# Agent attention and a routed MoE in one kernel: leftover rows read in place, row copies due later, queries and keys at other steps

## The chip, the cores and the metric

The kernel runs on one core of one Trainium2 chip, in one launch. The metric is the device time of the execution in microseconds (us). Three runs of the kernel before took 1318.40, 1320.83 and 1327.73 us; the median is 1320.83 us. The execution that was profiled took 1319.42 us, and its span from the first to the last instruction was 1317.7 us.

TensorE (PE) multiplies matrices, VectorE (DVE), ScalarE (ACT) and GpSimd (POOL) work on elements, and SyncE (SP) issues nearly all transfers of this kernel, one after the other in its program order. PEld is the load of a weight into PE, and it overlaps PE.

## The reference

There are 4 batches of 11456 tokens with 128 features, 49 agents for each batch, and 8 experts with 1024 hidden units.

```
scale = 1/sqrt(128)
def sm(a, b):                      # softmax over the last axis
    s = scale * (a @ b.T);  s = s - s.max(-1);  e = exp(s)
    return e / (e.sum(-1) + 1e-9)

agent_v = sm(agents, k) @ v        # 49 x 128 for a batch
x       = sm(q, agents) @ agent_v  # 11456 x 128 for a batch

logits = x @ w_gate                # all 45824 tokens
e      = argmax(logits);  g = softmax(logits)[e]
out    = g * (relu(x @ w1[e]) @ w2[e])
```

All inputs and the output are float32.

## The kernel before, in words

**Chunks, groups and steps.** A batch has 12 chunks: 11 of 1024 tokens (8 tiles of 128), and one of 192 tokens (2 tiles of 96). A chunk has up to two groups of 512 tokens, 23 groups in a batch. A group is worked off in 8 steps, one for each 128 hidden units, so that a batch takes 184 steps and a full chunk 16. The step is the unit of the kernel's own timetable.

**What a step does.** Most tokens of a batch are routed to one expert; its first weight is folded with `agent_v`, so that the first layer is a product of the exponentials of the query scores with a matrix `W` of 128 rows. The exponentials of the 49 agents are kept as float16 pairs, a high and a low part. The 128 rows that PE contracts at once (a tile `M`) hold 49 + 49 rows of the pair, and in the 30 left the high parts again, for the low part of the weight. The other 19 agents' high parts do not fit. For them there is a second, small product with 19 rows (`Wq`), in four groups of rows that start at rows 0, 32, 64 and 96: function `rests`, L1190, one group for each of four hidden tiles. Its input `Q` was four copies of 19 rows of `M` (L602). Then L1198 adds the product with 128 rows, ACT (L1203) and DVE (L1204) write the hidden units as a pair `hh`, and 5 steps later 12 matmuls (L1217) add them to the output `py`. After 8 steps DVE scales the group (`yo`, L1230) and SP stores it (issued by a helper's line, L1293).

**From queries to `M`.** A chunk of queries is loaded (L277), split into float16 pairs by ACT (L337) and DVE (L339), turned over by a transposing transfer `hT<-hl` on SP (L361), and multiplied with the agents on PE (L388 to L390). `qscores` and `qexp` (DVE L573, ACT L578) make the exponentials `E`, which SP also stores (`exps<-E`, L1293). `esplit` writes the pair into one of two buffers `mm` (DVE L584, ACT L585, DVE or POOL L587), `eturn` turns it over with another transposing transfer `M<-mm` (L593), `rest` issues the four copies `Q<-M`, and `logits` multiplies `M` with the gate's weights on PE (L610), for the routing. Keys of the next batch take the same way up to their scores, and stand beside the queries of the batch at hand.

**What sets the order.** The program is written out by a table of events: `at(t, f)` puts a function at step t, `after(dt, f)` puts it dt steps later than now. Each engine then works in its program order. The constants are steps. Queries of chunk c start at QA + 8c (first three chunks) and then every 13 steps (10.5 in the last batch), relative to the batch's step 0. Their scores come 9 steps later (KL), `esplit` another 3, and `logits` LL = 9.5 steps after the scores (LLL = 11 in the last batch). `rest` follows `eturn` by DTQ = 3.5 steps. Stores of `E` and of `yo` come DEX = 2 and DST = 2 steps after they are written. Keys of a next batch start at step -208 + 10c relative to that batch, which is step -24 + 10c of the batch at hand. For the second batch the first three keys thus stood ahead of step 0 of the first.

PSUM has 8 banks; six are for scores, logits and the first layer (`ph`, `ps_small`), two for `py`. There are 6 buffers of `M`, 3 of `Q`, and 2 of `hT` for keys and for queries each.

## Time and profile before

| what | us |
|---|---|
| median of three runs | 1320.83 |
| the profiled execution | 1319.42 |
| its span | 1317.7 |
| up to the first step of the first batch | 111 |
| the 736 steps of four batches | 111 to 1258 |
| blocks of tokens routed elsewhere, after that | 1258 to 1318 |

Times in the rows are from the start of the span. Busy time of an engine is a union of its instructions; PE's is stretched where its granted clock is low. A wait is idle time of an engine before an instruction, put down to what ended it. All of SP's work is issuing, so its rows in the timeline show how long the queue was taken by each issue.

### The profile page before, as it was taken

The page shows a single profiled execution, that of the slowest core. Times are in us where ns is not written, and L with a number is a line of the kernel's source. Part 1 is how long each engine was busy: PE and PEld are TensorE (multiplying, and loading weights), DVE is VectorE, ACT ScalarE, POOL GpSimd, SP SyncE. Part 2 cuts the span into 40 slices and gives each one's busy share as a digit, 9 for nine tenths or more (in the row PEclk, how much of TensorE's full clock was granted, in tenths as well). Part 3 has the DMA queues.
Part 4 walks back from the last instruction along what each step waited for, and adds up shares of the span by engine and source line. Part 5 has one row for each costly group of instructions (what it writes and reads, how often), then busy time and mean ns, then how long its engine had stood idle before and what let it go on. Part 6 is the DMA issues. An engine that isn't in the chain of part 4 may idle for free.

```text
span 1317.7 us, 35023 instructions
## 1 busy us (share of the span) xinstructions
PE 1074.8 (82%) x14238; PEld 832.7 (63%) x14238; DVE 1000.1 (76%) x2454; ACT 773.1 (59%) x1393; POOL 138.8 (11%) x198
## 2 busy tenths in 40 slices
PE   8626778789986877888987776888998879989995
PEld 8514557667764755666765665666775656667795
DVE  3677767687796786687887785768797968979985
ACT  4457646465486574566476583556476545666682
POOL 0200000032000000021200000012200012210123
PEclk9767888889997797999997797878998979988998
DMA  8769998643298798844189999743156576443270
GB/s 323 212 165 198 230 175 172 102 134 81 88 245 164 143 217 157 186 124 113 39 259 159 174 192 192 163 118 90 36 188 120 95 129 148 82 140 121 70 252 15
DMA packets 269813, 197.94 MB, mean 150 GB/s; under 512 B 218313, under 2 KB 231106, under 8 KB 269648
## 3 DMA queue, kind: packets, MB, share of 16 engines
q1 hardware_dynamic: 267792, 192.36, 63.2%
q0 software_dynamic: 1568, 2.25, 1.0%
q8 instruction: 113, 1.85, 0.6%
q10 hardware_dynamic: 288, 1.05, 0.3%
q14 instruction: 52, 0.43, 0.1%
HBM read 99.75 MB, written 36.43 MB: 103 GB/s over the span
## 4 chain that ended last, share of the span: by engine, by line
PE 34%; DMA 22%; DVE 21%; ACT 10%; issue 8%; SPq 3%; POOL 2%; POOLq 0%; ACTq 0%; DVEq 0%
PE py L1217 16%; DVE hh L1204 8%; PE ph L1198 7%; DMA M<-mm 7%; DMA ld<-in_q_dram 4%; PE ph L1190 4%; ACT hh L1203 3%; DMA wn<-in_moe_w_dram 3%; DMA hT<-hl 3%; DVE hl L339 2%; PE ps_small L478 2%; ACT jk L321 2%; DVE S L450 2%; DMA ld<-in_k_dram 2%; ACT hl L337 2%
## 5 line engine op out<-in xcount | busy, mean ns | idle before, releaser
L1217 PEld LDWEIGHTS <-hh 128*128 128x128 f16 x8640 | 584.5, 104 | 115.3 <-issue 40.0
L1217 PE MATMUL py<-w2h,hh 128*128 128x128 f16 (+1 forms) x5760 | 649.9, 229 | 1.4 <-ACT hh L1203 1.0
L1203 ACT ACTIVATE hh<-ph 128x512 f16<-128x512 f32 (+1 forms) x728 | 415.2, 585 | 304.1 <-PE ph L1198 275.0
L1204 DVE SCALAR_TENSOR_TENSOR hh<-ph,hh 128x512 f16<-128x512 f32 (+1 forms) x736 | 482.2, 669 | 145.4 <-ACT hh L1203 141.2
L1217 PE MATMUL py<-w2l,hh 128*128 128x128 f16 (+1 forms) x2880 | 559.5, 228 | 0.0
L1198 PE MATMUL ph<-M,W 128*128 128x512 f16 (+1 forms) x736 | 298.3, 409 | 0.0
L1190 PE MATMUL ph<-Q,Wq 19*128 19x512 f16 (+1 forms) x736 | 128.4, 401 | 90.0 <-DVE hh L1204 64.2
L1198 PEld LDWEIGHTS <-W 128*128 128x128 f16 x736 | 74.2, 102 | 115.0 <-issue 114.0
L321 ACT ACTIVATE jk<-ld 128x1024 f16<-128x1024 f32 (+1 forms) x84 | 84.8, 1010 | 56.7 <-DMA ld<-in_q_dram 35.8
L339 DVE SCALAR_TENSOR_TENSOR hl<-ld,mul,hl 128x1024 f16<-128x1024 f32 (+1 forms) x84 | 101.3, 1211 | 3.8 <-ACT hl L337 3.7
L337 ACT ACTIVATE hl<-ld,mul 128x1024 f16<-128x1024 f32 (+1 forms) x84 | 91.1, 1095 | 19.1 <-DMA hT<-hl 12.9
L388 PE MATMUL ps_small<-agh,hT 128*128 128x49 f16 (+1 forms) x630 | 62.9, 191 | 24.4 <-DMA hT<-hl 24.4
L587 POOL TENSOR_TENSOR mm<-E,mm 128x392 f16<-128x392 f32 (+1 forms) x18 | 14.7, 817 | 618.6 <-DVE mm L584 390.5
L1190 PEld LDWEIGHTS <-Wq 19*128 19x128 f16 x736 | 27.9, 92 | 80.6 <-issue 41.7
L610 PE MATMUL ps_small<-Gs,M 128*128 128x18 f16 x360 | 17.0, 174 | 74.8 <-DMA M<-mm 74.0
L388 PEld LDWEIGHTS <-hT 128*128 128x128 f16 (+1 forms) x630 | 56.0, 102 | 28.0 <-DMA hT<-hl 25.6
L610 PEld LDWEIGHTS <-M 128*128 128x128 f16 x360 | 14.0, 101 | 79.0 <-DMA M<-mm 78.2
L1230 DVE TENSOR_TENSOR yo<-py,cs 128x512 f32<-128x512 f32 (+1 forms) x92 | 61.4, 667 | 1.8 <-PE py L1217 1.6
L389 PE MATMUL ps_small<-agl,hT 128*128 128x49 f16 (+1 forms) x630 | 62.2, 190 | 0.0
L390 PE MATMUL ps_small<-agh,hT 128*128 128x49 f16 (+1 forms) x630 | 62.0, 190 | 0.0
L389 PEld LDWEIGHTS <-hT 128*128 128x128 f16 (+1 forms) x630 | 55.0, 102 | 1.6 <-issue 1.5
L390 PEld LDWEIGHTS <-hT 128*128 128x128 f16 (+1 forms) x630 | 54.3, 101 | 0.0
(295 smaller groups left out, 1313.1 us busy)
## 6 DMA issues: line engine op xcount, KB each, us to landing
ld<-in_k_dram SPq DMA_DIRECT2D x44, 512.0 KB
ld<-in_v_dram SPq DMA_DIRECT2D x44, 512.0 KB
ld<-in_q_dram SPq DMA_DIRECT2D x44, 512.0 KB
out_dram<-yo SPq DMA_DIRECT2D x88, 256.0 KB
w1e<-in_moe_w_dram SPq DMA_DIRECT2D x17, 512.0 KB
w2e<-in_moe_w_dram SPq DMA_DIRECT2D x17, 512.0 KB
exps<-E SPq DMA_DIRECT2D x44, 196.0 KB
wn<-in_moe_w_dram SPq DMA_DIRECT2D x16, 512.0 KB
```

The costliest lines, as they stand in the source:

```text
L321: nc.scalar.activation(jk[:p, :t * D], x[:p, :t, :].rearrange("p t d -> p (t d)"), AF.Square, accum_out=ss[:p])
L337: nc.scalar.activation(hi[:p, :t, :], x[:p, :t, :], AF.Copy, scale=m)
L339: nc.vector.scalar_tensor_tensor(lo[:p, :t, :], x[:p, :t, :], m, hi[:p, :t, :], op0=ALU.mult, op1=ALU.subtract)
L388: nc.tensor.matmul(o, x[:, 0, i, :p], AG["h"], start=True, stop=False)
L389: nc.tensor.matmul(o, x[:, 0, i, :p], AG["l"], start=False, stop=False)
L390: nc.tensor.matmul(o, x[:, 1, i, :p], AG["h"], start=False, stop=True)
L1190: nc.tensor.matmul(ph[:, :nn], st['Wq'][k, f0 // 4, :], st['Q'][c][k, h:h + n, :chunks[c][1]], start=True, stop=False)
L1198: nc.tensor.matmul(ph[:, :nn], st['W'][:, f, :], st['M'][c][:, h:h + n, :chunks[c][1]], start=False, stop=True)
L1203: nc.scalar.activation(hh[:, 0, :nn], ph[:, :nn], AF.Relu)
L1204: nc.vector.scalar_tensor_tensor(hh[:, 1, :nn], ph[:, :nn], 0.0, hh[:, 0, :nn], op0=ALU.max, op1=ALU.subtract)
L1217: mm_ = lambda l, r, **k: nc.tensor.matmul(o, l, r, skip_group_check=True, **k)
L1230: nc.vector.tensor_tensor(yo[:p, :n, :], py[:p, :n * D].rearrange("p (i d) -> p i d", d=D), cs.unsqueeze(2).broadcast_to([p, n, D]), op=AL ...
```

## The change

The 128 rows of `mm` are laid out anew: low parts in columns 0 to 48, high parts in columns 66 to 114 (UP = 66), and the 30 repeated high parts in two pieces, columns 49 to 65 (agents 0 to 16) and 115 to 127 (agents 17 to 29). Agents 30 to 48 thus lie in rows 96 to 114 of `M`, where the fourth row group of the small product reads its input in place. `rest` issues three copies, from rows 96 to 114, and has its own event: 9 steps (QD) ahead of the chunk's first step, or later. ACT repeats the 30 columns in two casts; the folded matrix `av` and the masks of rows follow the new layout.

The timetable changes too: queries 6 steps sooner (QA -20 to -26); LL 9.5 to 14 and LLL 11 to 15; DEX 2 to 4 and DST 2 to 5; and the keys of the second batch at step 3 + 7.6c of the first (KS1).

```diff
--- before.py
+++ after.py
@@ -22,6 +22,8 @@
 P = 128
 A = 49
 KR = 128 - 2 * A
+UP = 96 - KR
+DUP = ((A, 0, UP - A), (UP + A, UP - A, KR))
 CH = 1024
 BIG = float(1 << 20)
 UNROLL = 4
@@ -47,13 +49,13 @@
 VE, T1, TF0, TF1, TL, TLM, Q0 = 12, 1.75, 3, 1.5, 18, 10, 2
 
 KS, KT, VT, VL, VL4, TW0, TW1, DW = -208, 10, 4, 4, 4, 8, 2.5, 1
-QA, QB, QC, QB3, KL, LL, RG, D1, DL = -20, 8, 13, 10.5, 9, 9.5, 0.7, 0.5, 0
-
-KS1 = []
-
-KLL, LLL = 11, 11
-
-DTR, DTE, DTQ, DEX, DST, DXS = 2, 0.5, 3.5, 2, 2, 0.5
+QA, QB, QC, QB3, KL, LL, RG, D1, DL = -26, 8, 13, 10.5, 9, 14, 0.7, 0.5, 0
+
+KS1 = [3 + 7.6 * c for c in range(12)]
+
+KLL, LLL = 11, 15
+
+DTR, DTE, QD, DEX, DST, DXS = 2, 0.5, 9, 4, 5, 0.5
 
 LAG = 5
 
@@ -123,10 +125,14 @@
     pidx = cpool.tile([P, 1], F32, name="pidx")
     nc.gpsimd.iota(itmp[:, 0:1], pattern=[[0, 1]], base=0, channel_multiplier=1)
     nc.vector.tensor_copy(pidx, itmp[:, 0:1])
+    restrow = cpool.tile([P, 1], F32, name="restrow")
+    for o, a0, a1 in DUP:
+        nc.vector.tensor_scalar(itmp[:, 1:2].bitcast(F32), pidx, float(o), None, op0=ALU.is_ge)
+        nc.vector.tensor_scalar(itmp[:, 2:3].bitcast(F32), pidx, float(o + a1 - a0), None, op0=ALU.is_ge)
+        nc.vector.tensor_tensor(itmp[:, 3 + (a0 > 0):4 + (a0 > 0)].bitcast(F32), itmp[:, 1:2].bitcast(F32), itmp[:, 2:3].bitcast(F32), op=ALU.subtract)
+    nc.vector.tensor_tensor(restrow, itmp[:, 3:4].bitcast(F32), itmp[:, 4:5].bitcast(F32), op=ALU.add)
     sumrow = cpool.tile([P, 1], F32, name="sumrow")
-    nc.vector.tensor_scalar(sumrow, pidx, float(2 * A), None, op0=ALU.is_lt)
-    restrow = cpool.tile([P, 1], F32, name="restrow")
-    nc.vector.tensor_scalar(restrow, pidx, float(2 * A), None, op0=ALU.is_ge)
+    nc.vector.tensor_scalar(sumrow, restrow, -1.0, 1.0, op0=ALU.mult, op1=ALU.add)
     eidx = cpool.tile([P, E], F32, name="eidx")
     itmp2 = cpool.tile([P, E], I32, name="itmp2")
     nc.gpsimd.iota(itmp2, pattern=[[1, E]], base=0, channel_multiplier=0)
@@ -502,9 +508,10 @@
                 av = wpool.tile([P, P], F32, tag="av", name="av")
                 pt = small_ps()
                 nc.tensor.matmul(pt[:, :A], AV["acc"][:64 + A], both[:64 + A], start=True, stop=True)
-                nc.vector.tensor_tensor(av[:, :2 * A].rearrange("p (j a) -> p j a", a=A), pt[:, :A].unsqueeze(1).broadcast_to([P, 2, A]),
-                                        rs.unsqueeze(1).broadcast_to([P, 2, A]), op=ALU.mult)
-                nc.vector.tensor_copy(av[:, 2 * A:], av[:, :KR])
+                nc.vector.tensor_tensor(av[:, :A], pt[:, :A], rs, op=ALU.mult)
+                nc.vector.tensor_copy(av[:, UP:UP + A], av[:, :A])
+                for o, a0, a1 in DUP:
+                    nc.vector.tensor_copy(av[:, o:o + a1 - a0], av[:, a0:a1])
                 avq = one.tile([P, 4, 32], F32, tag="avq", name="avq")
                 nc.gpsimd.memset(avq, 0.0)
                 nc.gpsimd.tensor_copy(avq[:, :, :A - KR], av[:, KR:A].unsqueeze(1).broadcast_to([P, 4, A - KR]))
@@ -581,10 +588,12 @@
         def esplit(c):
             _, p, t = chunks[c]
             e, m2 = Es[c], mm[c % len(mm)]
-            nc.vector.tensor_copy(m2[:p, :t, :A], e[:p, :t, :])
-            nc.scalar.copy(m2[:p, :t, 2 * A:], e[:p, :t, :KR])
+            up = m2[:p, :t, UP:UP + A]
+            nc.vector.tensor_copy(up, e[:p, :t, :])
+            for o, a0, a1 in DUP:
+                nc.scalar.copy(m2[:p, :t, o:o + a1 - a0], e[:p, :t, a0:a1])
             eng = nc.gpsimd if pick(M2L if last else M2E, c) == "P" else nc.vector
-            eng.tensor_tensor(m2[:p, :t, A:2 * A], e[:p, :t, :], m2[:p, :t, :A], op=ALU.subtract)
+            eng.tensor_tensor(m2[:p, :t, :A], e[:p, :t, :], up, op=ALU.subtract)
             after(0 if first and c == 0 else DTE, eturn, c, m2)
 
         def eturn(c, m2):
@@ -592,14 +601,13 @@
             m = mpool.tile([P, 8, P], F16, tag="M", name="M")
             nc.sync.dma_start_transpose(m[:, :t, :p], m2[:p, :t, :].rearrange("p t a -> p (t a)"))
             Ms[c] = m
-            after(0 if first and c == 0 else DTQ, rest, c)
 
         def rest(c):
 
             _, p, t = chunks[c]
             x = Qs[c] = mpool.tile([P, 8, P], F16, tag="Q", name="Q", bufs=MQ)
-            for r in range(4):
-                nc.sync.dma_start(x[32 * r:32 * r + A - KR, :t, :p], Ms[c][KR:A, :t, :p])
+            for r in range(3):
+                nc.sync.dma_start(x[32 * r:32 * r + A - KR, :t, :p], Ms[c][96:96 + A - KR, :t, :p])
 
         def logits(c):
             _, p, t = chunks[c]
@@ -806,6 +814,7 @@
             at(base + t + ql_ + 3, esplit, c)
             tl = max(t + ql_ + (TL if first and c < NQ else LLL if last and c > 2 else LL), ta + (TLM if first else 4) + c / 2)
             at(base + tl, logits, c)
+            at(base + max(c * 16 - QD, t + ql_ + 6.5), rest, c)
             if c + 1 in starts or c == NCK - 1:
                 turns(route(c), base + tl + 1, RG, 6)
                 tf = max(tl + 1 + 6 * RG, tw + 1)
@@ -1187,7 +1196,8 @@
             for r in range(4):
                 k = slice(32 * r, 32 * r + A - KR)
                 ph = phs[g, f0 + r] = psH.tile([P, 512], F32, tag="h", name="ph")
-                nc.tensor.matmul(ph[:, :nn], st['Wq'][k, f0 // 4, :], st['Q'][c][k, h:h + n, :chunks[c][1]], start=True, stop=False)
+                nc.tensor.matmul(ph[:, :nn], st['Wq'][k, f0 // 4, :], st['Q' if r < 3 else 'M'][c][k, h:h + n, :chunks[c][1]],
+                                 start=True, stop=False)
 
         def layer1(g, f):
             c, h, n = groups[g]
```

Lines behind the first piece of the diff move by 6 to 10: L361 becomes L367, L388 L394, L593 L602, L602 L610, L610 L618, L1190 L1199, L1198 L1208, L1293 L1303.

How the program's order moves shows at two places. The first is PE at the start, from the last logits of the first batch's first three chunks (`Gs,M`) to its first step (`Wq`, `W`). Before:

```order
L610 MATMUL ps_small<-Gs,M 128x18
L293 MATMUL ps_small<-sa,ones 128x1
L303 MATMUL ps_small<-ident,ag 128x49
L388 LDWEIGHTS hT
L388 MATMUL ps_small<-agh,hT 128x49
L389 LDWEIGHTS hT
L389 MATMUL ps_small<-agl,hT 128x49
L390 LDWEIGHTS hT
L390 MATMUL ps_small<-agh,hT 128x49
```

and so on through two chunks of keys (48 matmuls), and only then the first step. In the change:

```order
L618 MATMUL ps_small<-Gs,M 128x18
L1199 LDWEIGHTS Wq
L1199 MATMUL ph<-Q,Wq 128x512
L1199 LDWEIGHTS Wq
L1199 MATMUL ph<-Q,Wq 128x512
L1199 LDWEIGHTS Wq
L1199 MATMUL ph<-Q,Wq 128x512
L1199 LDWEIGHTS Wq
L1199 MATMUL ph<-M,Wq 128x512
L1208 LDWEIGHTS W
L1208 MATMUL ph<-M,W 128x512
```

The keys' scores have gone behind the first step, and the fourth small product reads `M`.

The second is SP in the second batch, about the sixth chunk of queries, from its `exps` to the next. Before:

```order
L1293 DMA exps<-E 128x392
L1293 DMA out_dram<-yo 128x512
L593 DMA_TRANSPOSE M<-mm_137 128x8x128
L361 DMA_TRANSPOSE hT<-hl 128x16x128
L602 DMA Q<-M 19x1024 x4
L277 DMA ld<-in_q_dram 96x256
L277 DMA ld<-in_v_dram 128x1024
L1293 DMA out_dram<-yo 128x512
```

In the change:

```order
L1303 DMA exps<-E 128x392
L602 DMA_TRANSPOSE M<-mm_143 128x8x128
L367 DMA_TRANSPOSE hT<-hl 128x16x128
L610 DMA Q<-M 19x1024
L367 DMA_TRANSPOSE hT<-hl 128x16x128
L610 DMA Q<-M 19x1024
L1303 DMA out_dram<-yo 128x512
L610 DMA Q<-M 19x1024
```

The store no longer stands between the exponentials and `M<-mm`, and the copies are three, apart from each other, with a transpose between them. Over the whole program, counted in these rows, 29 of the 77 transposes `hT<-hl` that stand for a whole chunk had copies `Q<-M` among the transfers since the transpose ahead of them; now 38 have.

## Rows read from the trace of the kernel before

**Rows 1.** The page's first part: busy time of three engines (share of the span) and their instructions.

```profile
PE 1074.8 (82%) x14238; PEld 832.7 (63%) x14238; DVE 1000.1 (76%) x2454; ACT 773.1 (59%) x1393; POOL 138.8 (11%) x198
```

**Rows 2.** Stretches of the span, by batch: length, busy us of PE, PEld, DVE, ACT and POOL with counts, granted clock (share of 2.4 GHz), DMA share, GB/s.

```profile
0.00:111.00 111.00, 59.44 (x630) 54.24 (x630) 63.84 (x211) 54.33 (x92) 10.17 (x24) 0.76 0.80 223
111.00:400.00 289.00, 243.25 (x3338) 186.24 (x3336) 219.84 (x501) 178.28 (x323) 27.26 (x45) 0.91 0.71 161
400.00:700.00 300.00, 248.54 (x3375) 189.70 (x3375) 230.75 (x545) 181.78 (x329) 26.08 (x44) 0.90 0.70 157
700.00:1000.00 300.00, 250.55 (x3326) 190.77 (x3326) 227.94 (x539) 178.58 (x320) 26.54 (x43) 0.87 0.65 143
1000.00:1258.00 258.00, 229.29 (x2858) 168.96 (x2858) 217.09 (x596) 148.32 (x281) 30.07 (x28) 0.91 0.51 110
```

**Rows 3.** What PE waited for over the whole span: us in total, times, longest us.

```profile
PE ps_small L610 <- DMA M<-mm: 74.0, 23, 7.3
PE ph L1190 <- DVE hh L1204: 64.2, 52, 7.1
...
PE ph L1190 <- DMA Q<-M: 14.5, 10, 5.0
```

**Rows 4.** The same view for the stretches 111 to 400, 400 to 700, 700 to 1000 and 1000 to 1258 us, in this order: PE's waits for `M` ahead of the logits.

```profile
PE ps_small L610 <- DMA M<-mm: 13.9, 5, 5.4
...
PE ps_small L610 <- DMA M<-mm: 21.8, 6, 5.6
...
PE ps_small L610 <- DMA M<-mm: 21.8, 5, 7.3
...
PE ps_small L610 <- DMA M<-mm: 8.4, 5, 3.3
```

**Rows 5.** Timeline of PE ahead of the first step: start us, us, what, and in brackets the idle time before it and what ended that.

```profile
91.92 0.34 PE L303 MATMUL ps_small<-ident,ag 49*128 49x49 f32 x1
107.21 0.22 PE L388 MATMUL ps_small<-agh,hT 128*128 128x49 f16 x1 [14.95 <-DMA hT<-hl]
...
109.94 0.22 PE L388 MATMUL ps_small<-agh,hT 128*128 128x49 f16 x1 [1.55 <-DMA hT<-hl]
...
111.06 0.61 PE L1190 MATMUL ph<-Q,Wq 19*128 19x512 f16 x4
```

**Rows 6.** Timeline of the same stretch on SP (two rows) and on DVE (one row, the last weight of the second layer).

```profile
78.94 3.03 SPq L602 DMA_DIRECT2D Q<-M  x4
...
95.50 11.80 SPq L361 DMA_TRANSPOSE hT<-hl  x2
```

```profile
86.64 1.28 DVE L743 SCALAR_TENSOR_TENSOR w2l<-w2e,pinv,w2h 128x1024 f16<-128x1024 f32 x1
```

**Rows 7.** Timeline of SP in the second batch, without a row left out: start us, us that the issue took, what.

```profile
478.07 0.41 SPq L1293 DMA_DIRECT2D out_dram<-yo  x1
478.52 6.37 SPq L361 DMA_TRANSPOSE hT<-hl  x1
484.94 1.52 SPq L277 DMA_DIRECT2D ld<-in_v_dram  x3
486.56 5.50 SPq L361 DMA_TRANSPOSE hT<-hl  x1
492.14 0.53 SPq L1293 DMA_DIRECT2D exps<-E  x1
492.76 0.38 SPq L1293 DMA_DIRECT2D out_dram<-yo  x1
493.25 1.29 SPq L593 DMA_TRANSPOSE M<-mm  x1
494.59 2.64 SPq L361 DMA_TRANSPOSE hT<-hl  x1
497.32 2.45 SPq L602 DMA_DIRECT2D Q<-M  x4
```

**Rows 8.** Timeline of the same chunk on the other engines: the last part of `esplit` (POOL), the logits (PE), and the group `yo` (DVE) whose store is the first of rows 7.

```profile
485.19 0.91 POOL L587 TENSOR_TENSOR mm<-E,mm 128x392 f16<-128x392 f32 x1 [43.39 <-DVE mm L584]
```

```profile
496.70 0.39 PE L610 MATMUL ps_small<-Gs,M 128*128 128x18 f16 x8 [5.59 <-DMA M<-mm]
```

```profile
465.48 0.68 DVE L1230 TENSOR_TENSOR yo<-py,cs 128x512 f32<-128x512 f32 x1
```

**Rows 9.** Instructions by line: count, shortest/median/longest ns, first and last start in us. The first row holds one matmul for each step.

```profile
L1198 PE MATMUL ph<-M,W x736: 242/379/634, 111.6 to 1257.9; 128*128 128x512 f16 x176, 128*128 128x192 f16 x8
```

```profile
L602 SPq DMA_DIRECT2D Q<-M x192: 561/562/1129, 78.9 to 1217.0; - x192
```

```profile
L585 ACT CAST mm<-E x48: 230/384/466, 74.4 to 1160.9; 128x240 f16<-128x240 f32 x44, 96x60 f16<-96x60 f32 x4
```

**Rows 10.** One copy of `av`'s columns on DVE (timeline), and a copy `Q<-M` on the chain of waits (start us, us to its landing).

```profile
58.39 0.17 DVE L507 COPY av<-av 128x30 f32<-128x30 f32 x1
```

```profile
399.84 6.02 DMA Q<-M
```

## The prediction

> **What bounds the kernel now.** I read the busy times first, then the stretches by batch, then PE's waits, and last SP's timeline where PE waits. No engine is full: PE is busy 82% of the span, DVE 76%, ACT 59% [rows 1]. In the second and third batch PE works 249 and 251 of 300 us, DVE 231 and 228 [rows 2], so each loses some 50 us in gaps. PE's list of waits names them: 74.0 us in 23 waits for `M` ahead of the logits, 64.2 us in 52 short waits for a `ph` bank that DVE's `hh` gives back, and 14.5 us for `Q` [rows 3]. The first of these lies, but for 8 us ahead of the first step, in the four batches: 13.9, 21.8, 21.8 and 8.4 us, together 65.9 us [rows 4].
>
> Why `M` is late is read off one chunk. `esplit` ends at 485.19 + 0.91 = 486.10 [rows 8], but SP issues `M<-mm` only at 493.25, because from 478.07 to 499.77 its issues follow each other almost without a gap: the nine rows add up to 21.1 of 21.7 us [rows 7]. `M` lands 3.45 us later, when PE has stood for 5.59 us [rows 8]. So in the query part of a batch it is the in-order SP queue, full of transposes, that ends last; PE's order places the logits at a fixed number of steps behind `esplit`, too few for it. A step takes (1257.9 - 111.6) / 736 = 1.56 us on average [rows 9].
>
> The other place is the start. PE is done with the logits and one small transpose at 91.92 + 0.34, stands 14.95 us until keys of the *second* batch have been turned over, 1.55 us for the next such chunk, and takes the first step at 111.06 [rows 5]. The step itself could have gone: the first chunk's `Q` copies were issued by 78.94 + 3.03, the last weight was written at 86.64 + 1.28 = 87.92 [rows 6].
>
> **The change part by part.** The sum is made against the profiled execution, 1319.4 us; the median of the runs is 1.4 us above it.
>
> *Keys behind the first step.* PE's order now goes from the logits straight to the first step, so the 111.06 - 92.26 = 18.8 us fall away. What is moved isn't saved: the two key transposes that held SP for 11.80 us [rows 6] now stand in a queue that is also busy behind step 0, and the keys follow at 7.6 steps in place of 10, some three more chunks within the first 87 steps. Ends: 18.8 us (SP's later gaps take them) and 18.8 - 11.8 = 7 us. I take the middle, 13 us, since DMA share in the first batch is 0.71 [rows 2] and later steps have room.
>
> *Logits later, queries sooner.* Between `esplit` and the logits there are now 4.5 steps more (4 in the last batch), 4.5 x 1.56 = 7.0 us. The longest wait for `M` is 7.3 us, the mean of the 21 in the batches 3.1 us, so counted in steps nearly all 65.9 us go. `M` is also freed from a store that stood ahead of it and waited for `yo`. But the transposes don't get shorter: where SP is 97% occupied a faster PE runs into it again. Ends: 66 us, and a third, 20 us, if SP alone sets the pace. I take three quarters, 49 us: queries begin 6 steps sooner, in the part of a batch where SP has gaps, and the queue has the rest of the batch to catch up. The routing that follows the logits has steps to spare before its first store, so it isn't late next; what is next is `hh`, below.
>
> *Three copies, due 9 steps ahead.* SP saves 48 issues of 0.562 us [rows 9], 27 us over the run, where it is full. Against that stands how transposes fare behind copies: the one behind four copies and a store took 6.37 us, the one behind a transpose 2.64 us [rows 7], 3.7 us apart; by the program's order 38 in place of 29 stand behind copies. If the price hangs on standing there, that is 9 x 3.7 = 33 us more, and SP is 6 us worse off; if on nothing, 27 us better. I take a small relief and book none of it: it is in the three quarters above. The rows can't tell whether three copies cost a transpose as much as four. The Trainium skill, "DMA: Bandwidth & Descriptors", section "Why a DMA increments its semaphore by 16 and not by 1", says that a copy is spread over the largest number of engines, up to 16, that divides its slowest dimension; for 19 rows that is one engine. By that rule the 3.7 us are one engine working off the copies, and go with their number: 29 x 3.7 = 107 us become 80, SP is 54 us better off, the whole 66 us come back, and the time would be 1243; no row here shows the single engine. Of PE's 14.5 us for `Q` [rows 3], which come mostly at a batch's first chunk, I take 10 us back (ends 14.5 and, in a rival below, a loss).
>
> *Stores later.* `exps` and `yo` go out 2 and 3 steps later. SP then finds them ready. They have no reader close by and three buffers, 24 steps, of `yo`; I book nothing. If a buffer were to run short, DVE's next `yo` would wait for the store, 6 us or so (as a copy's landing [rows 10]) in 8 steps.
>
> *New layout.* ACT makes two casts of 17 and 13 columns for one of 30, 0.384 us [rows 9]: 48 more, between 0 and 0.384 us each, at most 18 us on an engine with 41% idle, and inside 7 us of new slack; 0. `av` costs DVE two more copies of 0.17 us [rows 10] in each of four batches and some six tiny mask operations at the start: 2 us as a bound, and I take all of it. The fourth small product reads other rows of the same size: 0. I assume that DVE's writes at column 66 go at the speed of those at 0; no row shows it.
>
> *What is late next.* When PE stands less, DVE must turn out `hh` in less time. At 280 us for a batch DVE would be 231 / 280 = 82% busy. The waits for `hh` are 1.2 us each now; ten more a run for early chunks, 10 us given back.
>
> Sum: 13 + 49 + 10 - 2 - 10 = 60 us, hence 1319.4 - 60 = 1259, with the median's 1.4 us **1260 us**. Own range with the terms' ends: 1225 (all 99 us of the start, `M` and `Q` come back, less some for `hh`) to 1280.
>
> **The rivals.**
>
> *The stall moves to `hh` (25%).* PE no longer waits for `M`, but at the next `ph` bank for DVE, which has 77% of a batch and a burst of splits, maxima and `hh` in the query part. For it: 64.2 us already wait there [rows 3]. Against it: most of those are short and follow other gaps. Then a third of the 66 us comes back: 13 + 22 + 5 - 10 = 30 us, 1290 us.
>
> *SP is the bound and nothing but the start moves (10%).* The slack is eaten since `M` is issued as late, in steps, as before: every transpose stays, and nine more stand behind copies. For it: 97% [rows 7]. Against it: only the query part is like that. The start's lower end, 7 us, and some 3 us for `Q`: 1310 us.
>
> *The copies come too late (8%), slower.* `Q` used to be issued long ahead of use, but for a batch's first chunk; now 9 steps, 14.0 us, ahead by the timetable. SP runs behind: `yo` of one group was ready at 466.16 [rows 8] and its store, due 2 steps (3.1 us) later, issued at 478.07 [rows 7], 8.8 us late. Issuing three copies takes 1.8 us, landing 6.02 us [rows 10]; 14.0 - 8.8 - 1.8 - 6.0 = -2.6 us, PE waits 2.6 us. For the first seven chunks of four batches, 28 x 2.6 = 73 us on the wrong side: 1260 + 73 = 1333 us. It decides once SP is more than 6.2 us behind. Against it: the lateness comes from the load that the change spreads out, and copies may stand further ahead in SP's order than the table asks. The Trainium skill, "DMA: Bandwidth & Descriptors", section "Rules for kernel authors", advises the opposite of this edit, to issue a transfer early and wait late; the trace agrees as far as PE now waits for `Q` where the copies came last, 14.5 us.
>
> **How the numbers follow.** The forecast has 57%, the rivals 25, 10 and 8%. The range runs from 1225 to 1304, past the second case with its own spread, and leaves out the third, the fourth and a thin lower tail, some 20%. 1% of 1320.8 us, 13 us, is about what a measurement of this kernel tells from no change. Faster by more than that: the forecast, nearly all of the first rival and little else, 82%; within 1%: most of the second rival and the edge of the first, 11%; slower: 7%.
>
> **What would show it.** Right: the first `Wq` matmul at 90 to 98 us; PE's waits for `M` below 20 us in place of 74.0; the four batches some 45 to 50 us shorter together. Wrong: waits for `M` above 45 us (SP is the bound); waits for `hh` above 100 us (the first rival); waits for `Q` above 30 us, in many chunks (the last); transposes behind copies still at 6.2 us and more in SP's timeline speak against the relief there.

## The result, and the profile after

In the same session the kernel before took 1318.40, 1320.83, 1327.73 and 1348.77 us, and the changed one 1287.95 us (median; 1286.01 to 1291.87, 4 runs): a ratio of 0.9744, 95% interval 0.9690 to 0.9797, 34 us less. Executions sometimes fall into a slower state, some 2% longer, as the 1348.77 us did, and the ratios are of the others alone; two profiles below, whose start was lengthened in this way, have their total and first step in brackets. The forecast was 1260 us with a range of 1225 to 1304. The profiled execution of the change took 1286.95 us, its span is 1285.3 us. Ratios to the kernel before, not medians, are compared below.

The first view is PE's waits over the whole span of the changed kernel, to be held against [rows 3]: us in total, times, longest.

```profile
PE ps_small L394 <- DMA hT<-hl: 53.3, 18, 5.5
PE ph L1199 <- DVE hh L1214: 45.3, 49, 6.3
PE ps_small L618 <- DMA M<-mm: 34.2, 7, 6.6
```

The waits for `M` are less than half of what they were (34.2 us, 8.7 of them ahead of the first step), those for `Q` are gone from the list, and those for `hh` have shrunk. The scores (L394) now stand first: they wait 53.3 us for `hT`. Before, this row stood third, in the place of the dots in [rows 3], and 15.0 of its 24.4 us were the one wait ahead of the first step:

```profile
PE ps_small L388 <- DMA hT<-hl: 24.4, 7, 15.0
```

The same view for the four batches, 89.0 to 378.4, to 678.1, to 974.6 and to 1225.7 us, against [rows 4]:

```profile
PE ps_small L618 <- DMA M<-mm: 13.7, 3, 6.2
PE ps_small L394 <- DMA hT<-hl: 10.3, 4, 4.7
...
PE ps_small L394 <- DMA hT<-hl: 18.1, 6, 5.2
...
PE ps_small L618 <- DMA M<-mm: 6.6, 1, 6.6
...
PE ps_small L394 <- DMA hT<-hl: 18.0, 6, 5.5
...
PE ps_small L618 <- DMA M<-mm: 5.2, 1, 5.2
...
PE ps_small L394 <- DMA hT<-hl: 3.4, 1, 3.4
```

In the batches the waits for `M` fell from 65.9 to 25.5 us, and those for `hT` rose from 3.9 (in the trace of before, batch by batch 0, 1.6, 1.8 and 0.5) to 49.8 us. PE still waits for transposes; only the place differs.

The four batches as one stretch, from the first step to the last, before and after (length, busy us of PE, PEld, DVE, ACT and POOL, granted clock, DMA share, GB/s):

```profile
111.60:1257.90 1146.30, 970.94 (x12893) 735.45 (x12890) 895.52 (x2178) 686.30 (x1251) 109.94 (x160) 0.90 0.65 144
```

```profile
89.00:1225.70 1136.70, 976.42 (x12945) 735.53 (x12942) 899.10 (x2237) 698.78 (x1307) 114.12 (x160) 0.91 0.66 147
```

The first step begins at 89.0 in place of 111.6 us, 22.6 us earlier, and the batches together are 9.6 us shorter: these two make the difference of the spans, 32.4 us. In the batches PE's idle time (length less busy time) fell by 15.1 us, from 175.4 to 160.3, and its busy time rose by 5.5 us; the trace has 52 more matmuls there, about the number of the two chunks of keys that used to stand ahead of the first step. The PE timeline ahead of the first step shows that the keys' waits of [rows 5] are gone from there; the one wait left is for the third chunk's `M`:

```profile
88.10 0.38 PE L618 MATMUL ps_small<-Gs,M 128*128 128x18 f16 x8 [5.35 <-DMA M<-mm]
88.42 0.61 PE L1199 MATMUL ph<-Q,Wq 19*128 19x512 f16 x3
```

Last, SP in the second batch, which answers to [rows 7] (start us, us that the issue took, what):

```profile
451.60 1.99 SPq L367 DMA_TRANSPOSE hT<-hl  x1
453.69 0.66 SPq L610 DMA_DIRECT2D Q<-M  x1
454.45 3.85 SPq L367 DMA_TRANSPOSE hT<-hl  x1
458.35 0.61 SPq L610 DMA_DIRECT2D Q<-M  x1
459.05 0.35 SPq L1303 DMA_DIRECT2D out_dram<-yo  x1
459.46 0.60 SPq L610 DMA_DIRECT2D Q<-M  x1
460.11 0.42 SPq L283 DMA_DIRECT2D ld<-in_v_dram  x1
460.63 6.67 SPq L367 DMA_TRANSPOSE hT<-hl  x1
...
481.89 1.86 SPq L610 DMA_DIRECT2D Q<-M  x3
483.85 5.17 SPq L367 DMA_TRANSPOSE hT<-hl  x1
```

A transpose behind no copy took 1.99 us here, behind one 3.85, behind three 5.17. "Behind three copies" means: with three copies `Q<-M` among SP's transfers since the transpose ahead. Over the whole trace the median of a transpose `hT<-hl` of a whole chunk is 3.71 us behind one copy (7 of them), 5.31 behind two (8), 5.17 behind three (21), and before it was 6.29 behind four (25). Copies are not all that makes one long: the 39 behind no copy have a median of 3.43 us, 3.87 for the 22 with a load `ld` among the transfers since the transpose ahead and 2.17 for the 17 without, and the 6.67 us above stand behind two copies, a store and a load. Where nothing but copies was issued since the transpose ahead, the medians are 2.17, 3.78, 4.68 and 5.15 us for none, one, two and three (13, 4, 2 and 3 cases), and before 6.22 for four (3): roughly 1 us more for each copy. SP spent 332.2 us on the 77 transposes of whole chunks before and 299.7 after.

### The profile page after: what moved, and what is told of

It is laid out like the page before. It is cut to its first block, busy times and chain, and to the rows that moved or that the text cites. A ratio compares the mean times of both kernels' runs of the same rounds, so it can differ in the third digit from the quotient of the medians.

```text
span 1285.3 us, 35032 instructions
## 1 busy us (share of the span) xinstructions
PE 1077.1 (84%) x14238; PEld 829.8 (65%) x14238; DVE 990.9 (77%) x2468; ACT 777.2 (60%) x1441; POOL 143.0 (11%) x198
## 5 line engine op out<-in xcount | busy, mean ns | idle before, releaser
L1208 PE MATMUL ph<-M,W 128*128 128x512 f16 (+1 forms) x736 | 295.2, 405 | 0.0
L1208 PEld LDWEIGHTS <-W 128*128 128x128 f16 x736 | 73.5, 102 | 105.5 <-issue 104.5
L1199 PE MATMUL ph<-Q,Wq 19*128 19x512 f16 (+1 forms) x552 | 104.8, 400 | 33.6 <-DVE hh L1214 31.0
L327 ACT ACTIVATE jk<-ld 128x1024 f16<-128x1024 f32 x84 | 85.1, 1013 | 43.1 <-DMA ld<-in_q_dram 29.3
L394 PE MATMUL ps_small<-agh,hT 128*128 128x49 f16 x630 | 62.2, 190 | 54.8 <-DMA hT<-hl 53.3
L345 DVE SCALAR_TENSOR_TENSOR hl<-ld,mul,hl 128x1024 f16<-128x1024 f32 x84 | 102.3, 1220 | 6.4 <-ACT hl L343 6.2
L1199 PE MATMUL ph<-M,Wq 19*128 19x512 f16 (+1 forms) x184 | 74.6, 405 | 28.9 <-DVE hh L1214 14.2
L343 ACT ACTIVATE hl<-ld,mul 128x1024 f16<-128x1024 f32 x84 | 91.3, 1098 | 8.4 <-DVE mul L212 8.3
L394 PEld LDWEIGHTS <-hT 128*128 128x128 f16 x630 | 54.9, 101 | 59.3 <-DMA hT<-hl 56.8
L596 POOL TENSOR_TENSOR mm<-E,mm 128x392 f16<-128x392 f32 (+1 forms) x18 | 17.9, 993 | 559.1 <-DVE mm L592 550.2
L1199 PEld LDWEIGHTS <-Wq 19*128 19x128 f16 x736 | 29.8, 92 | 65.6 <-issue 35.8
L396 PE MATMUL ps_small<-agh,hT 128*128 128x49 f16 x630 | 61.9, 190 | 0.0
L395 PE MATMUL ps_small<-agl,hT 128*128 128x49 f16 x630 | 61.9, 190 | 0.0
L578 DVE TENSOR_REDUCE mq<-ps_small 128x8 f32<-128x392 f32 (+1 forms) x48 | 25.6, 533 | 44.1 <-PE ps_small L396 40.7
L395 PEld LDWEIGHTS <-hT 128*128 128x128 f16 x630 | 54.3, 101 | 2.6 <-issue 2.4
L396 PEld LDWEIGHTS <-hT 128*128 128x128 f16 x630 | 54.0, 100 | 0.0
```

Of the source, the lines that this page charges most:

```text
L327: nc.scalar.activation(jk[:p, :t * D], x[:p, :t, :].rearrange("p t d -> p (t d)"), AF.Square, accum_out=ss[:p])
L343: nc.scalar.activation(hi[:p, :t, :], x[:p, :t, :], AF.Copy, scale=m)
L345: nc.vector.scalar_tensor_tensor(lo[:p, :t, :], x[:p, :t, :], m, hi[:p, :t, :], op0=ALU.mult, op1=ALU.subtract)
L394: nc.tensor.matmul(o, x[:, 0, i, :p], AG["h"], start=True, stop=False)
L395: nc.tensor.matmul(o, x[:, 0, i, :p], AG["l"], start=False, stop=False)
L396: nc.tensor.matmul(o, x[:, 1, i, :p], AG["h"], start=False, stop=True)
```

## The experiments

The table has every kernel in one place: the ratio to the kernel before in the same session, the profiled execution, and from its trace the start of the first step, the length of the four batches, and SP's time on the 77 transposes `hT<-hl` of whole chunks. Times are in us.

| kernel | copies x rows | ratio (95%) | profiled us | first step | four batches | `hT` on SP |
|---|---|---|---|---|---|---|
| before | 4 x 19 | 1 | 1319.4 | 111.6 | 1146.3 | 332.2 |
| the change | 3 x 19 | 0.974 (0.969 to 0.980) | 1287.0 | 89.0 | 1136.7 | 299.7 |
| keys alone | 4 x 19 | 0.996 (0.993 to 0.999) | 1312.9 | 88.8 | 1162.8 | 333.8 |
| keys back | 3 x 19 | 0.990 (0.986 to 0.995) | 1303.4 | 108.7 | 1134.2 | 300.4 |
| queries and logits back | 3 x 19 | 0.965 (0.956 to 0.974) | 1272.9 | 90.2 | 1121.1 | 289.9 |
| logits back | 3 x 19 | 0.965 (0.960 to 0.970) | 1273.4 | 89.4 | 1121.3 | 301.9 |
| copies soon | 3 x 19 | 0.964 (0.956 to 0.971) | 1276.6 | 87.5 | 1126.3 | 291.3 |
| stores back | 3 x 19 | none | (1304.3) | (114.2) | 1128.9 | 295.1 |
| four copies | 4 x 19 | 0.993 (0.989 to 0.997) | 1307.0 | 90.8 | 1153.1 | 314.9 |
| 23 rows | 3 x 23 | 0.997 (0.992 to 1.001) | 1319.7 | 89.6 | 1169.2 | 319.8 |
| 20 rows | 3 x 20 | 0.919 (0.914 to 0.924) | 1214.2 | 86.7 | 1066.1 | 223.9 |
| 32 rows | 3 x 32 | 0.912 (0.905 to 0.918) | (1229.6) | (112.2) | 1055.7 | 224.9 |
| 32 rows, queries and logits back | 3 x 32 | 0.915 (0.909 to 0.920) | 1210.3 | 87.2 | 1062.8 | 236.7 |
| 32 rows in the kernel before | 4 x 32 | 0.927 (0.921 to 0.934) | 1225.5 | 102.3 | 1063.1 | 237.0 |

### The keys: alone, and taken out of the change

The kernel before with one line of the change:

```diff
-KS1 = []
+KS1 = [3 + 7.6 * c for c in range(12)]
```

> The kernel before, with the second batch's keys moved behind the first step and nothing else. Theory A (the start gave most of the gain: the first step went from 111.6 to 89.0 us in the change, and the four batches together became only some 10 us shorter): first step at 89 to 92 us, 20 to 23 us faster than before, 1298 to 1301 us. Rival B (the moved keys are paid back in the first batch, where SP is full, and the gain needs the other edits): first step as early, but the first batch longer by 8 us or more, 1305 to 1315 us.

Ratio 0.996, some 5 us, or 6.5 by the profiled executions. The first step came 22.8 us sooner, but the first batch grew from 291.3 to 305.4 us: alone, the edit is mostly paid back, as rival B said (its time, 1305 to 1315 us, is missed by a little). The first batch before and here:

```profile
111.60:402.90 291.30, 243.15 (x3336) 186.12 (x3332) 220.66 (x507) 177.71 (x322) 27.26 (x45) 0.91 0.71 159
88.80:394.30 305.50, 251.37 (x3388) 189.10 (x3384) 231.70 (x559) 185.66 (x333) 28.23 (x45) 0.89 0.73 164
```

PE's busy time there is 8.2 us longer, with 52 more matmuls and a lower granted clock, and its idle time 6.0 us. So SP is not alone in taking the gain back. Its part is seen in PE's waits for `M` in that batch, 13.9 us before [rows 4]:

```profile
PE ps_small L610 <- DMA M<-mm: 21.1, 4, 8.9
```

The reverse, the change with `KS1 = []`:

> The change, with the second batch's keys back ahead of the first step. Theory A: first step back at 108 to 112 us, 20 to 23 us slower than the change, 1306 to 1311 us. Rival B: the other edits carry the gain, 1288 to 1297 us.

Ratio 0.990 against 0.974, as theory A said: inside the change the keys are worth some 21 us (0.016 of 1326), 16.5 us by the profiled executions. The first step falls back by 19.7 us, and the batches are only 2.5 us shorter without the moved keys. So the same edit is worth some 6 us alone and 16 to 21 us next to the other edits. That these give it room by taking transposes' time off SP (332.2 to 300.4 us) is likely, but no run tries it by itself.

### The timetable: queries, logits, copies, stores

The change with both of its edits on queries and logits taken back:

```diff
-QA, QB, QC, QB3, KL, LL, RG, D1, DL = -26, 8, 13, 10.5, 9, 14, 0.7, 0.5, 0
+QA, QB, QC, QB3, KL, LL, RG, D1, DL = -20, 8, 13, 10.5, 9, 9.5, 0.7, 0.5, 0
-KLL, LLL = 11, 15
+KLL, LLL = 11, 11
```

> The change, with queries and logits back at their old steps (QA -20, LL 9.5, LLL 11). Theory C (SP's queue of transposes sets the pace in the query part, and the wait only changes its name): PE's waits for M in the batches rise from 25 to 50 us or more, waits for hT fall from 50 to 20 us or less, and the time moves by less than 8 us: 1284 to 1296 us. Rival D (the slack is worth what was forecast, and something else in the change cost as much): 30 us or more slower, 1318 us or above.

Ratio 0.965: below both ranges, and faster than the change by about 1%. In the four batches PE's waits and their whole stretch are:

```profile
PE ps_small L618 <- DMA M<-mm: 59.7, 17, 8.8
PE ps_small L394 <- DMA hT<-hl: 13.4, 5, 5.2
```

```profile
90.20:1211.30 1121.10, 964.36 (x12944) 727.74 (x12941) 900.73 (x2237) 697.15 (x1307) 111.87 (x160) 0.92 0.66 149
```

Theory C's marks are met: the wait changes its name. `M` and `hT` together are 73.1 us, 75.3 in the change, and PE's idle time is 156.7 us, 160.3 in the change. So the edit on which the forecast rested gained nothing, and seems to cost about 1%. To part its two halves, the logits alone were put back (LL 9.5 and LLL 11, QA left at -26):

> The change with the logits at their old distance from the scores (LL 9.5, LLL 11), the queries left at 6 steps sooner. With both taken back the time fell by some 12 us, and this run parts the two. Theory Q (the sooner queries press the transposes into a full queue, and later logits do no harm): PE's waits for M grow to 50 us and more in the batches, time 1285 to 1305 us. Rival R (the later logits are what costs, since they put off the routing and its row work): 1270 to 1280 us. Rival S (both wait for the same transposes, so that what PE doesn't wait at one place it waits at the other): 1280 to 1292 us, waits for M plus hT as in the change, about 75 us in the batches.

Ratio 0.965 again, so the sooner queries by themselves make no difference that can be told. PE's waits in this kernel:

```profile
PE ps_small L618 <- DMA M<-mm: 84.7, 21, 8.7
PE ps_small L394 <- DMA hT<-hl: 36.4, 12, 5.0
PE ph L1199 <- DVE hh L1214: 34.9, 48, 5.4
```

So the later logits do what they say: with them the waits for `M` are 34.2 us, without them 84.7. But the kernel with 50 us more of these waits is the faster one, by 13.5 us of the profiled executions. Its four batches as one stretch:

```profile
89.40:1210.70 1121.30, 960.82 (x12944) 729.04 (x12941) 901.51 (x2237) 695.79 (x1307) 113.96 (x160) 0.92 0.66 149
```

PE's idle time there is 1121.3 - 960.8 = 160.5 us, against 1136.7 - 976.4 = 160.3 in the change: the sum of all gaps is the same. That holds for all gaps, and not for these two waits alone, as rival S had it; in the four batches they are

```profile
PE ps_small L618 <- DMA M<-mm: 75.9, 19, 8.7
PE ps_small L394 <- DMA hT<-hl: 33.0, 11, 5.0
```

together 108.9 us in place of 75.3, while waits for `hh` and others are smaller. The 15.4 us lie in PE's busy time, which is 15.6 us less at a mean granted clock of 0.92 in place of 0.91. Over the whole span the clock was 0.912 to 0.913 in this kernel's three runs and 0.902 to 0.906 in the change's four, so this is no chance of one execution. The range that held, 1270 to 1280, was given with another reason, that later logits put off the routing; no run shows that. Why the clock is granted more freely when the same idle time lies at the logits stays open.

The copies back at 3.5 steps behind `M`'s transpose:

```diff
+            after(0 if first and c == 0 else 3.5, rest, c)
-            at(base + max(c * 16 - QD, t + ql_ + 6.5), rest, c)
```

> The change with the copies of Q issued 3.5 steps after M's transpose, as before, in place of 9 steps ahead of their use. Theory L (copies lump together again ahead of one transpose each, and steps' worth of M and hT are held by them either way): within 8 us of the change, 1280 to 1296 us. Rival M (late copies, apart from each other, are the part of the change that shortened the batches): 1296 to 1315 us. Rival N (late copies put 38 in place of 29 transposes behind copies, and cost): 1265 to 1280 us.

Ratio 0.964, in the range of the theory that late copies cost. 30 transposes stand behind copies in this trace, 38 in the change, and SP's time on them falls by 8.4 us; the batches are 10.4 us shorter.

The stores back at their old steps (`DEX, DST = 2, 2`):

> The change with the stores at their old steps (exps 2 and yo 2 steps after they are written, in place of 4 and 5). Theory O (SP's queue waits for yo and E at the stores' heads, 128.3 and 57.5 us in the change and more when the stores come sooner, and what stands behind waits too): 1295 to 1320 us. Rival P (the store's wait costs nothing, as the queue has other waits in its place): 1283 to 1293 us.

There is no ratio: a single run of 1278.99 us stands for this kernel. In the profiled execution the batches took 1128.9 us against 1136.7, so nothing here speaks for a gain by later stores; that they cost isn't shown either, as a single run is no interval.

Each of the three kernels with an interval lies about 1% below the change (0.965, 0.965 and 0.964 against 0.974). The upper ends of their intervals reach 0.974, 0.970 and 0.971, the lower end of the change's is 0.969, so for each alone this is at the edge of what the measurement tells. All three are held against the same four runs of the change, so they are not three independent signs.

### The number of copies

The change with the fourth copy put back (`range(4)`, and the fourth row group reads `Q`):

> The change with a fourth copy of 19 rows again: rows 96 to 114 of M are copied four times, and the fourth row group reads Q. Theory E (each copy of 19 rows holds a transpose behind it by about a quarter of 5 us): SP issues 48 more copies at 0.56 us, 27 us, and hT behind four copies takes 6.3 to 7 us in place of 5.17 behind three, some 1.3 us for each of 38 transposes, 50 us; where SP is the bound most of it shows: 1310 to 1350 us. Rival K (three copies hold a transpose as long as four, so that only the issues are saved): 1290 to 1310 us.

Ratio 0.993, which is 1310 us, where the two ranges meet: reading the fourth group in place is worth about 0.018, 24 us. The transposes decide between the theories. Their median behind four copies is 6.25 us (17 of them), against 5.17 behind three, so a fourth copy does hold a transpose longer, by 1.08 us. SP's time on transposes grew by 15.2 us, though, not by the 50 that theory E worked out; its 48 more issues took 26.7 us.

### The number of rows in a copy

What makes a copy so dear was tried by its rows alone. In each of these the copy takes more rows than are read, so it moves more bytes. The change with 32 rows:

```diff
-                nc.sync.dma_start(x[32 * r:32 * r + A - KR, :t, :p], Ms[c][96:96 + A - KR, :t, :p])
+                nc.sync.dma_start(x[32 * r:32 * r + 32, :t, :p], Ms[c][96:128, :t, :p])
```

> The change, with each copy of leftover rows made 32 rows wide (rows 96 to 127 of M; 13 more rows that nothing reads) in place of 19. Theory E (a copy of 19 rows is worked off by one DMA engine, and a transpose behind it waits for that engine): with 32 rows spread over 16 engines, transposes hT behind three copies fall from a median of 5.2 us to 4 us or less, their sum from 300 us to 270 us or less, PE's waits for hT fall, and the time falls by 8 to 25 us, to 1263 to 1280 us. Rival F (the price is for standing behind copies, or for the bytes): 68% more bytes, transposes behind copies as long or longer, time the same or up to 10 us slower.

Ratio 0.912, some 1204 us, far more than expected. The median transpose behind three copies took 2.05 us. 32 rows also fill a block of partitions and are more bytes, so two kernels parted the reasons: 20 rows, which ten divides, and 23, a prime as 19 is. The same line with `+ 20` and `[96:116]`:

> The change, with each copy of Q 20 rows (96 to 115 of M) instead of 19; the one more row is read by nobody. Theory E (a copy goes to as many engines as the largest number up to 16 that divides its rows: 10 for 20 rows, 1 for 19): a transpose hT behind three copies takes at most 3 us on SP (5.17 in the change, 2.05 with 32 rows), all hT issues together 220 to 250 us (299.7 in the change), and the time is 1195 to 1235 us. Rival F (32 rows help because they fill a whole block of 32 partitions, or because the copy is larger): 20 rows are like 19, hT behind three copies at 4.8 to 5.6 us, time 1275 to 1295 us.

and with `+ 23` and `[96:119]`:

> The change, with each copy of Q 23 rows (96 to 118 of M) instead of 19. 23 is a prime, so theory E expects one engine again and 23/19 of the work: hT behind three copies at 5.2 to 6.5 us on SP, time 1285 to 1330 us. Rival F (a wider copy is a faster one, without regard to what divides it): hT behind three copies at 3 to 4.5 us, time 1245 to 1280 us.

One row more takes 0.055 off the change's ratio (0.919 against 0.974), four rows more add 0.022 (0.997). Both kernels met theory E's marks and times. SP's timeline in the second batch with 20 rows:

```profile
450.85 2.30 SPq L610 DMA_DIRECT2D Q<-M  x3
453.26 1.74 SPq L367 DMA_TRANSPOSE hT<-hl  x1
```

and with 23 rows:

```profile
444.90 2.32 SPq L610 DMA_DIRECT2D Q<-M  x3
447.26 0.44 SPq L283 DMA_DIRECT2D ld<-in_k_dram  x1
447.81 6.15 SPq L367 DMA_TRANSPOSE hT<-hl  x1
```

The medians behind three copies are 1.95 us with 20 rows, 5.17 with 19 and 6.19 with 23 (21 transposes in each). Against 20 rows a copy of 19 rows thus holds the next transpose by (5.17 - 1.95) / 3 = 1.07 us, one of 23 rows by 1.41 us. Neither the bytes nor the width decides.

What does is seen in the packets. The trace doesn't name the engine of a packet, but it keeps each packet's start, length and size. One row of a copy is one packet of 2048 bytes. The table takes transposes that stand right behind all copies of a chunk, one of each kernel (the others of this kind have the same count at one time; overlaps of under 0.01 us aren't counted):

| rows, start of the transpose | packets of the copies | most at one time | their first start to last end, us | issue of the transpose, us | its end behind the last packet, us |
|---|---|---|---|---|---|
| 3 x 19, 483.85 | 57 | 1 | 5.65 | 5.17 | 0.21 |
| 3 x 23, 497.86 | 69 | 1 | 6.70 | 6.25 | 0.25 |
| 3 x 20, 453.26 | 60 | 10 | 1.93 | 1.74 | 0.80 |
| 3 x 32, 416.37 | 96 | 16 | 1.74 | 2.05 | 1.03 |
| 4 x 19 in the kernel before, 452.81 | 76 | 1 | 7.26 | 6.19 | 0.23 |

With 19 and 23 rows the packets go one after the other, and the transpose's issue ends 0.2 us behind the last of them; with 20 rows they go ten at a time, with 32 sixteen. It is what the Trainium skill, "DMA: Bandwidth & Descriptors", section "Why a DMA increments its semaphore by 16 and not by 1", says: the largest number up to 16 that divides the slowest dimension, so 1 for 19 and for 23, 10 for 20, 16 for 32. These runs agree with it in all four cases. Numbers of rows with a largest divisor between 1 and 10 weren't tried, and why the issue of a transpose waits for the packets ahead of it stays open.

The price in PE's terms, the four batches with 20 rows:

```profile
86.70:1152.80 1066.10, 954.58 (x12944) 721.29 (x12941) 897.87 (x2236) 696.24 (x1309) 112.20 (x160) 0.94 0.64 157
```

Against the change PE's idle time falls from 160.3 to 111.5 us, and its busy time by 21.8 us at a mean granted clock of 0.94 in place of 0.91. Over the whole span PE's longest waits are now for `hh`:

```profile
PE ph L1199 <- DVE hh L1214: 43.8, 50, 5.5
PE ps_small L394 <- DMA hT<-hl: 28.9, 15, 3.6
PE ps_small L618 <- DMA M<-mm: 11.3, 4, 4.6
```

With 32 rows, do the queries and logits still matter? QA -20, LL 9.5 and LLL 11 again:

> The change with copies of 32 rows and with the queries and logits at their old steps (QA -20, LL 9.5, LLL 11). Theory G (queries sooner costs only because it piles transposes and slow copies into one stretch of SP's queue; with short copies there is nothing to pile up): within 10 us of the change with copies of 32 rows alone, whose undisturbed runs took 1200 to 1210 us, so 1190 to 1220 us. Rival H (the sooner queries cost by themselves, 11 us as with copies of 19 rows): 1180 to 1195 us. Rival I (with short copies SP follows the table, so that the later logits do save PE's waits for M): 1220 us and more, with PE's waits for M above 30 us in the batches.

Ratio 0.915 against 0.912: no difference that can be told, as theory G said. Rival I's mark is there, 37.6 us of waits for `M` in the batches, but not its time: with 32 rows and the later logits PE waits 24.5 us for `hT` and 4.7 for `M`, here 4.3 and 37.6. And the kernel before, with nothing but its four copies widened:

```diff
-                nc.sync.dma_start(x[32 * r:32 * r + A - KR, :t, :p], Ms[c][KR:A, :t, :p])
+                nc.sync.dma_start(x[32 * r:32 * r + 32, :t, :p], Ms[c][KR:KR + 32, :t, :p])
```

> The kernel before, with each of its four copies of Q 32 rows (30 to 61 of M) instead of 19; nothing else of the change. Theory E: hT behind four copies falls from 6.29 us to 2 to 3.5 us on SP, and the time to 1230 to 1275 us, most of it out of the 65.9 us that PE waits for M in the batches. Rival J (before, the table puts the logits too few steps behind esplit whatever SP does): PE's waits for M stay at 50 us or more in the batches, time 1295 to 1325 us.

Ratio 0.927, a little below the first theory's range. The transposes behind four copies went from 6.29 to 2.05 us, SP's time on transposes from 332.2 to 237.0 us. PE's waits:

```profile
PE ph L1190 <- DVE hh L1204: 44.2, 56, 4.9
PE ps_small L610 <- DMA M<-mm: 43.9, 20, 4.9
PE ps_small L388 <- DMA hT<-hl: 14.6, 4, 7.4
```

38.3 us of the waits for `M` lie in the batches, 27.6 less than before: the rival with 50 us or more falls, though not all of them go; the logits still stand 9.5 steps behind the scores here. The four batches as one stretch:

```profile
102.30:1165.40 1063.10, 949.39 (x12893) 719.49 (x12890) 893.38 (x2180) 686.56 (x1254) 109.35 (x160) 0.94 0.65 159
```

They are 83.2 us shorter, by an edit that saves not one instruction; 61.7 us of it is PE's idle time (175.4 to 113.7), the rest its busy time (970.9 to 949.4).

## Why the prediction was right in its range and wrong in its sum

**The time.** 1287.95 us lies inside the range and faster by over 1%, 28 us above the forecast. In the profiled executions 32.4 us came back of the 60 forecast, and not where the sum put them: 22.6 us at the start, for which it had 13, and 9.6 in the batches, for which it had 47. None of the three marks of being right was met (the first `Wq` matmul came sooner, waits for `M` were 34.2 us, the batches 9.6 us shorter), and of those of being wrong only the last in part: single transposes behind copies still took more than 6.2 us, as the 6.67 above. That the time lies in the range is due to the width of the range and to the start, and in this is luck.

**Keys behind the first step, 13 us (7 to 18.8).** The place was right and the size low: the first `Wq` matmul at 88.42 us (forecast 90 to 98), 22.6 us sooner, of which 16 to 21 us stay. That the logits would be done some 4 us sooner as well was not counted. Alone the edit keeps some 6 us, close to the lower end. This end took the 11.8 us of moved transposes as paid again in a full queue; in "keys alone" more than half of what is paid back, 8.2 of 14.1 us in the first batch, is PE's own busy time, which the step left out.

**Logits later, queries sooner, 49 us.** This is the step that failed. Three quarters of PE's waits for `M` were to come back; the waits fell by 40.4 us in the batches, and the scores' waits for `hT` rose by 45.9. The step noted that a faster PE runs into SP again, gave 20 us as the end for that case, and then took the other side. Even 20 was too much: with the edit taken back the kernel is, if anything, about 1% faster. The mistake was to price a wait at the place where PE meets it. What ended last was SP's transposes, and moving the reader doesn't shorten them; PE's gaps in the batches sum to 160.3 us in the change, to 156.7 with queries and logits back, and to 160.5 with the logits back. Shorter transposes do close them: with 20 rows they are 111.5 us, and `M` and `hT` together 33.4 in place of 75.3.

**Three copies, booked at nothing (6 us worse to 27 better).** Worth about 24 us, by the run with four. The rows [rows 7] had 6.37 us behind copies against 2.64, and the sentence by the Trainium skill gave the reason; both were in the prediction, and the price was left at "the rows can't tell". The packets that show it were in the trace of the kernel before as well (76 of them one at a time, in the table above), so these would have told. The time by that rule, 1243, missed too, though not by what it gave SP: the 54 us there (27 of issues, 27 of transposes) came out as 23.7 and 32.5, if with 38 transposes behind copies in place of its 29. What failed is the next step, that with this all 66 us of PE's waits come back: PE's idle time in the batches fell by 15.1 us.

**Copies due later, no price.** Putting them back is worth some 1%, at the edge of what the measurement tells. PE's waits for `Q`, 14.5 us [rows 3], did go in the change, as booked (10 us), and no copy came too late: the slower rival falls. But more transposes behind copies are a cost that the step worked out, 33 us for nine at the dearest, and then dropped. In "copies soon" 30 stand there in place of 38, and SP has 8.4 us less of transposes. The Trainium skill's advice in "DMA: Bandwidth & Descriptors", section "Rules for kernel authors", to issue early, agrees with that run, though for another reason than a late landing.

**Stores later and the new layout, 0 and 2 us.** The stores' single run tells no cost, and no run tries the layout by itself, so its 2 us stay open.

**`hh` late next, 10 us given back.** It didn't happen: these waits fell from 64.2 to 45.3 us. The rival on `hh` gave 1290 us, close to the result, but not by its mechanism, whose mark was more than 100 us of these waits.

**SP is the bound (10%).** Its mark, waits for `M` above 45 us, wasn't met, since PE met the queue elsewhere; its mechanism is what held in the batches, 9.6 us shorter in place of 45 to 50. The mark should have been PE's waits for *any* transpose, 65.9 + 3.9 = 69.8 us before and 25.5 + 49.8 = 75.3 after, next to its whole idle time.

## What to carry to other kernels

When an engine waits for an in-order queue, add up its waits for everything that comes out of that queue, and its whole idle time in the stretch, before pricing an edit that moves one of the readers: here `M` lost 40 us, `hT` gained 46, and with the reader moved back the idle time was within 4 us of the same. Then ask of each issue in the queue why it is as long as it is, and whether the same issue is shorter elsewhere in the trace (6.37 against 2.64 us); that difference, and not the timetable, held the 96 us (0.073 of 1326) that wider copies alone gave the kernel before. Where the price is on a copy, count in the trace how many of its packets run at one time. Give a copy on chip a number of rows with a large divisor, if need be with rows that nobody reads: copying 32 or 20 rows for 19 takes 0.912 or 0.919 of the time before (the intervals overlap).

## What the runs showed of the hardware that was not expected

The cost of a copy falls on the transfer behind it. Its own issue takes a median of 0.605 us of SP with 19 rows in the change and 0.758 us with 20, so by the issues alone the 20-row copy is the dearer; the transpose issued next takes 5.17 us behind three of the one and 1.95 behind three of the other. The packets differ the other way from what their number suggests: a packet of the 19-row copy takes 0.084 us (median), one of the 20-row copy, with nine others beside it, 0.155, and still the three copies are done in 1.93 us in place of 5.65. And what the queue costs PE is more than its waits: between 19 and 20 rows 48.8 us of idle time and 21.8 us of busy time go together, at a mean granted clock of 0.91 and 0.94.
